# Turning x on TensorE instead of the DMA, half of r too, and another order and layout for the experts' loads

## The chip, the cores and the metric

The kernel runs on one core of one Trainium2 chip. The metric is device microseconds (us) of one execution. TensorE multiplies, VectorE (DVE in the profile), ScalarE (ACT) and GpSimd (POOL) do elementwise work, SyncE (SP) only issues transfers. All transfers run on the core's 16 DMA engines. A transpose of 128x128 blocks can be done in two ways here: by TensorE, which multiplies with the identity and leaves the result in PSUM, from where another engine copies it; or by a DMA transpose, which goes from SBUF to SBUF and takes 2-byte numbers only.

## The reference, cut to what matters

```python
# attention: 4 batches, 8 heads, 576 tokens, head_dim 64; only scores within tau of a row's maximum stay
scores = 1/8 * q @ k.T
attn   = softmax(where(scores >= scores.max(-1) - tau, scores, -1e9))
x      = (attn @ v)                      # put together as 2304 x 512
# a dense layer
h = x @ w_in                             # 512 -> 2048
x = maximum(0.01 * h, h) @ w_out         # 2048 -> 512
# soft mixture of 8 experts, 4 slots each
logits     = x @ phi                                     # 2304 x 32
slot_input = softmax(logits, axis=0).T @ x               # 32 x 512
slot_out[e] = maximum(slot_input[e] @ w1[e], 0) @ w2[e]  # w1: 8x512x1024, w2: 8x1024x512
out        = softmax(logits, axis=1) @ slot_out          # 2304 x 512
```

All inputs are float32 (w_in and w_out reach the chip as float64 bits and are converted there).

## The kernel before, in words

The 2304 tokens are 18 tiles of 128 rows. The program is one function, `emit`, which does not issue instructions in the order in which it names them: each step is put into a plan with a priority, one or more engines that may do it with an estimated duration, the buffers that it reads and writes, and a planner (`Plan.schedule`) lists them against modelled engines, a modelled DMA and the numbered buffers of each tag. The result is one fixed order for every engine, and every engine, SP's queue too, takes its list strictly in that order: an instruction that waits holds up all behind it.

Per tile, `attention(t)` loads q, computes the scores of eight heads on TensorE (L1089), takes the row maximum on DVE (L1102), the exponential on ACT (L1123), the threshold on DVE (L1130), and splits the result into a high and a low float16 half (ACT L1156, POOL L1166). Eight DMA transposes per tile (L1188, 9 blocks of 128 columns each) turn this into `aT`, and TensorE multiplies it with v (L1198) into the PSUM tile `X`.

Then comes the part that is changed. DVE divides X into `x32` (L1220, float32). ACT makes its float16 half (L1228), DVE or POOL the rest (L1231), and one DMA transpose of 8 blocks (L1238) makes `xT`. `feed(t)` multiplies xT with w_in in four chunks j of 512 columns (L1266, 12 matmuls each, into the PSUM tag `h`, which has two buffers). ACT applies the leaky ReLU (L1279) and makes the float16 half of `r[j]` (L1285), POOL or DVE the rest (L1288), and a DMA transpose of 8 blocks (L1311) makes `rT[j]`. TensorE multiplies the four rT[j] with w_out times phi (L1321, L1325) into the logits. `block` takes two tiles at a time and adds their share to the softmax over the tokens (L1381 to L1505). So a tile issues 8 + 1 + 4 = 13 DMA transposes, all of them on SP's queue, 234 in the whole run. From 100 to 545 us of the span this is the work of all engines; before it weights are converted, after it come the last two tiles and the experts.

The experts are bound to loads. `load` puts a piece of 256 KB into any free buffer of a large pool (tag list `CH`, many tags that the tiles use before). For w1 (L1702) a piece is 128 rows of 512 columns, a row of 2 KB; four experts write the four quarters of the partitions of one PSUM tile `h1`, in the order expert j outside, row block k inside. For w2 (L1773) a piece is 2 x 128 rows of half of the columns, 256 floats or 1 KB in a run; here expert j is already inside. There are 64 pieces of each. The output is made in two column halves `hf`, each after its 32 pieces of w2: evict (L1783), spread (L1786, L1789, L1791), 18 matmuls (L1802), evictions (L1809 on ACT, L1812 on DVE) and nine stores (L1820), each with runs of 1 KB. Stores of the first half are kept back in the plan until the last load is issued.

Of the kernel before, what the change touches and what calls it, by code (L numbers as in the profile page):

```python
# [341 lines left out]
def emit(tc, a, out, dbg=None, opt=None):  # L342
# [2 lines left out]
    ctx = ExitStack()  # L345
    pl = Plan()
    O = dict(
        LH=2.3, LB=2.6, HG=3, NR=13, NT=6, NW=5, XH=1, XT=4, KX=10, VX=5, AE=2, AH=3, AT=3, QH=2, QL=2,
        QR=2, TQ=("qr", "raw"), KR=2, VR=4, RAW=1, G=2, PO=0.3, PI=-8.0, PV=-3.0, DA=-100, TK=("kr",
        "w2"), TV=("vr", "kr"), TX=("kx", "w2"), TH=(0, 2), VP=1, MT=0, PS=0.15, NM=6, E=1, LA=2, MG=0,  # L350
        MH=0, RES=0, MI=(2, 1, 2, 1), MO=(1, 1, 1, 1), WT=("w",), PST=0, BH=1, DP={"vr": 1.0, "xT":
        0.1, "xh": 0.25, "X": -0.25, "kx": -1.0, "x32": 0.1, "g": 0.25, "E": -0.1, "S": -1.0, "h": 1.0,
        "r": 1.0, "rT": 0.5, "qr": 1.0, "ql": 0.25, "qh": 1.0, "ah": 0.5, "vx": -0.1, "misc": -1.0,
        "dh": -0.25, "kr": -0.25, "z": -0.1, "th": 0.5, "aT": -1.0}, LO=4, LP=2, PB=1, TU=("x32", "xh",
        "xT", "rT"), TO=("raw", "rT"), TE=18, TR=18, TG=("g",), BI={"spa": 300}, LG=0, CAP=(("aT",
        1),), PL=-0.5, TL=("rT", "xT", "ae"), NA=24, QU=(), CT=0, CX=("aT",), TW=("aT", "ql", "qh",
        "qr"), WQ=(),
    )
# [10 lines left out]
    def t_act(n):  # L369
        return 94 + 0.832 * n  # L370
# [40 lines left out]
    for n, p_, k in (  # L411
        ("S", "pss", 2), ("X", "psx", 1), ("h", "psh", 2), ("misc", "psm", 1),
        ("r", "main", O["NR"]), ("rT", "main", O["NT"]), ("w", "main", O["NW"]),
        ("x32", "main", 1), ("xh", "main", O["XH"]), ("xT", "main", O["XT"]),
        ("qr", "main", O["QR"]), ("qh", "main", O["QH"]), ("ql", "main", O["QL"]), ("kr", "main", O["KR"]),
        ("kx", "main", O["KX"]), ("vr", "main", O["VR"]), ("vx", "main", O["VX"]),
        ("ae", "main", O["AE"]), ("ah", "main", O["AH"]), ("aT", "main", O["AT"]),
        ("z", "main", 2), ("z1", "main", 2), ("rz", "main", 2), ("nm", "main", O["NM"]),
        ("th", "main", O["NM"]), ("sm", "main", 12), ("lg", "main", 3), ("E", "main", O["E"]),
        ("dh", "main", 2), ("sl", "main", 1), ("wh", "main", 16), ("g", "main", O["G"]), ("ls", "main", 2), ("g", "main", O["G"]), ("tmp", "main", 16), ("raw", "main", O["RAW"]),  # L420
    ):
        pl.tag(n, p_, k)
# [7 lines left out]
    def dve_op(prio, ns, fn, r=(), w=()):  # L430
        return pl.add(prio, one("dve", ns, fn), r, w)
# [4 lines left out]
    def pool_op(prio, ns, fn, r=(), w=()):  # L436
        return pl.add(prio, one("pool", ns, fn), r, w)
# [15 lines left out]
    def dump(name, b, sel, prio=1e9):  # L453
# [5 lines left out]
    ident, e4, e96, ones = const([P, P]), const([P, NS]), const([P, 3, NS]), const([1, P])  # L459
    pool_op(P0, 600, lambda: make_identity(nc, ident.ap), w=[ident])  # L460
    pool_op(P0, 150, lambda: pool.memset(ones.ap, 1.0), w=[ones])
    dve_op(
        P0, 250,
        lambda: dve.tensor_reduce(
# [672 lines left out]
    def attention(t):  # L1137
# [5 lines left out]
        for pr in range(4):  # L1143
# [40 lines left out]
            for i in range(2):  # L1184
# [58 lines left out]
        return xT, xh  # L1243

# [7 lines left out]
    def feed(t, xT, xh):  # L1252
# [4 lines left out]
        for j in range(4):  # L1257
# [37 lines left out]
            else:  # L1295
# [13 lines left out]
            dma_t(  # L1309
                p + 0.1, 8,  # L1310
                (lambda j: lambda: sp.dma_start_transpose(  # L1311
                    out=rT[j].ap, in_=r[j].ap.rearrange("p a b -> p (a b)")))(j),
                r=[r[j], wq], w=[rT[j]],
            )
# [439 lines left out]


    HC, firsts = DM // 2, []
    outv = out.rearrange("(t i p) d -> t p i d", i=2, p=P)
    so_ps = pl.buf("X", [P, 2, HC])
    for hf in range(2):
        pt = T0 + 2 + hf  # L1760
        cols = slice(hf * HC, hf * HC + HC)
        for G in range(2):
            for c in range(0, 8, 2):
                for j in range(4):
                    q = hts[G]
# [12 lines left out]

                    tail_op("pe", p, 262, f, r=[(q, (j, c // 4)), w], w=[(so_ps, j)])
# [16 lines left out]
        for t in range(0, NTILE, 2):  # L1796
# [8 lines left out]
            for i in range(2):  # L1805
# [29 lines left out]
def host(inputs):  # L1835
# [21 lines left out]

# [16 lines left out]
```

## Time and profile before

| | |
|---|---|
| median of 3 runs | 666.04 us (664.19 to 670.23) |
| profiled execution | 668.88 us |
| its span, first to last instruction | 667.1 us |
| busy in the span | PE 527.1, DVE 442.1, ACT 425.9, POOL 345.9 us |
| DMA | 145.26 MB, 316522 packets, of which 270624 under 512 B |
| mean granted TensorE clock | 0.934 of full speed |

Read it by stages: conversion of weights to about 100 us, the tiles to 545, the drain of the last two tiles and the softmax over tokens to 589, w1 to 627, w2 to 655, the last output to the end. PE is the busiest engine on average, but an average over these stages says little: what ends the waits in each stage says more.

### The profile page before, as it was taken

What the parts mean: (1) busy time and instruction counts of PE and PEld (TensorE: products, weight loads), DVE (VectorE), ACT (ScalarE), POOL (GpSimd) and SP (SyncE); (2) the same over time, 40 slices, a digit from 0 to 9 for tenths busy, and PEclk for the clock granted to TensorE, in tenths of its full rate; (3) what the DMA queues carried; (4) which work ended last, traced back from release to release, by engine and by line L of the source; (5) the groups of instructions that cost most, each with busy time, mean ns of one, the idle gap of its engine ahead of it and who ended that gap; (6) DMA issues with size and microseconds to landing.
All of it is one profiled execution on the core that took longest, in us unless ns stands there. A gap on an engine that the chain in (4) does not pass through costs nothing. (4 is left out here: it accounts for less than half of the span.)

```text
span 667.1 us, 15257 instructions
## 1 busy us (share of the span) xinstructions
PE 527.1 (79%) x5622; PEld 322.4 (48%) x5622; DVE 442.1 (66%) x1068; ACT 425.9 (64%) x806; POOL 345.9 (52%) x364
## 2 busy tenths in 40 slices
PE   0111787989799988889799989898979696499994
PEld 0011576666466545555465556565545453132553
DVE  6999978888678767878686976577776531201033
ACT  7999778776587776889677867575765542111022
POOL 3553445575676676868657877676774600000000
PEclk9999967989899999999699999799999897789998
DMA  8954889998999999999989999999998999899995
GB/s 304 338 212 123 201 227 217 249 198 183 168 192 236 190 172 186 178 211 213 182 162 189 189 155 192 207 186 168 171 156 144 256 224 242 283 381 348 365 311 196
DMA packets 316522, 145.26 MB, mean 218 GB/s; under 512 B 270624, under 2 KB 291616, under 8 KB 316448
## 3 DMA queue, kind: packets, MB, share of 16 engines
q1 hardware_dynamic: 309248, 130.56, 90.3%
q10 hardware_dynamic: 7200, 13.73, 8.3%
q8 instruction: 44, 0.72, 0.5%
q14 instruction: 30, 0.25, 0.1%
HBM read 69.27 MB, written 8.91 MB: 117 GB/s over the span
## 5 line engine op out<-in xcount | busy, mean ns | idle before, releaser
L1166 POOL TENSOR_TENSOR ah<-ae,ah 128x512 f16<-128x512 f32 (+1 forms) x216 | 206.4, 978 | 97.4 <-ACT ah L1156 72.2
L1266 PE MATMUL h<-wh,xT 128*128 128x512 f16 x864 | 217.4, 391 | 10.0 <-DMA xT<-xh 9.8
L1102 DVE TENSOR_REDUCE nm<-S 128x1 f32<-128x576 f32 x144 | 103.0, 748 | 62.7 <-PE S L1089 62.7
L1123 ACT ACTIVATE ae<-S,nm 128x576 f32<-128x576 f32 x144 | 100.8, 738 | 40.6 <-DVE nm L1102 32.9
L1266 PEld LDWEIGHTS <-xT 128*128 128x128 f16 x864 | 77.6, 101 | 91.3 <-issue 12.7
L1130 DVE SCALAR_TENSOR_TENSOR ae<-S,th,ae 128x576 f32<-128x576 f32 x144 | 113.7, 812 | 11.1 <-ACT ae L1123 10.3
L1198 PE MATMUL X<-vx,aT 128*128 128x64 f16 (+1 forms) x2240 | 94.2, 200 | 30.0 <-DMA aT<-ah 29.9
L1198 PEld LDWEIGHTS <-aT 128*128 128x128 f16 (+1 forms) x2240 | 82.4, 105 | 62.8 <-DMA aT<-ah 41.7
L1156 ACT ACTIVATE ah<-ae 128x576 f16<-128x576 f32 x144 | 96.0, 681 | 10.5 <-DVE ae L1130 8.9
L1089 PE MATMUL S<-kx,qh 64*128 64x288 f32 (+1 forms) x600 | 82.4, 340 | 6.8 <-DVE ae L1130 6.2
L1279 ACT ACTIVATE g<-h 128x512 f32<-128x512 f32 x72 | 42.9, 596 | 49.5 <-PE h L1266 42.7
L1089 PEld LDWEIGHTS S<-kx,qh 64*128 64x128 f32 (+1 forms) x600 | 56.0, 199 | 25.9 <-issue 21.5
L1288 POOL TENSOR_TENSOR r<-g,r 128x512 f16<-128x512 f32 x42 | 48.8, 1166 | 17.1 <-ACT r L1285 17.1
L1089 PE MATMUL S<-kx,ql 64*128 64x288 f32 (+1 forms) x280 | 48.3, 316 | 11.2 <-DVE ql L975 11.2
L1285 ACT ACTIVATE r<-g 128x512 f16<-128x512 f32 x72 | 45.0, 628 | 0.4
L1288 DVE TENSOR_TENSOR r<-g,r 128x512 f16<-128x512 f32 x30 | 28.9, 965 | 20.1 <-ACT r L1285 20.1
L1089 PEld LDWEIGHTS S<-kx,ql 64*128 64x128 f32 (+1 forms) x280 | 32.3, 202 | 11.6 <-DVE ql L975 11.6
L496 PE MATMUL misc<-c,tmp 128*1 128x128 f32 x16 | 4.5, 380 | 33.4 <-DVE tmp L563 30.0
L1321 PE MATMUL misc<-c,rT 128*128 128x64 f16 x288 | 19.0, 190 | 9.5 <-DMA rT<-r 9.5
L1321 PEld LDWEIGHTS <-rT 128*128 128x128 f16 x288 | 17.5, 97 | 12.2 <-DMA rT<-r 10.0
L799 PE MATMUL misc<-c,w 128*128 128x32 f32 x128 | 19.3, 298 | 4.4 <-DVE w L791 2.6
L1231 POOL TENSOR_TENSOR xh<-x,xh 128x512 f16<-128x512 f32 x12 | 14.4, 1200 | 15.3 <-ACT xh L1228 12.6
(334 smaller groups left out, 828.8 us busy)
## 6 DMA issues: line engine op xcount, KB each, us to landing
wh<-in_w SPq DMA_DIRECT2D x29, 256.0 KB, 6.4
r<-in_w SPq DMA_DIRECT2D x24, 256.0 KB, 5.2
rT<-in_w_out SPq DMA_DIRECT2D x22, 256.0 KB, 3.5
ah<-in_w_in SPq DMA_DIRECT2D x9, 512.0 KB, 5.9
kx<-in_w SPq DMA_DIRECT2D x16, 256.0 KB, 5.9
ae<-in_w_in SPq DMA_DIRECT2D x7, 512.0 KB, 4.3
vr<-in_v SPq DMA_DIRECT2D x10, 320.0 KB, 4.1
scr<-w SPq DMA_DIRECT2D x12, 256.0 KB, 3.9
```

Of the source, the lines that this page charges most:

```text
L1089: pe.matmul(out=pss[i].ap[:rows, n, :HALF], lhsT=l.ap[64 * i : 64 * i + 64, pr, :rows], rhs=m.ap[64 * i : 64 * i + 64, n * HALF : (n + 1) ...
L1102: lambda: dve.tensor_reduce(out=nm.ap, in_=ps.ap[:, :, :HALF], axis=AX.XY, op=ALU.max, negate=True),
L1123: lambda: act.activation(out=e(), in_=ps.ap[:, :, :HALF], func=AF.Exp, bias=nm.ap[:, 0:1], scale=1.0),
L1130: lambda: dve.scalar_tensor_tensor(out=e(), in0=ps.ap[:, :, :HALF], scalar=th.ap[:, 0:1], in1=e(), op0=ALU.is_ge, op1=ALU.mult, accum_out= ...
L1156: (lambda ah, ae, i: lambda: act.activation(out=ah.ap[:, i, :S], in_=ae.ap[:, i], func=AF.Copy))(ah, ae, i),
L1166: (lambda ah, ae: lambda: pool.tensor_tensor(out=ah.ap[:, h, w0 : w0 + c1 - c0], in0=ae.ap[:, h, c0:c1], in1=ah.ap[:, h, c0:c1], op=ALU.su ...
L1198: pe.matmul(out=X.ap[r0:r1, 2 * pr + i], lhsT=aT.ap[:, c, r0:r1], rhs=vtiles[b, pr].ap[:, wv, cv], start=(pr == 0 and i == 0 and n == 0), ...
L1266: pe.matmul(out=hp.ap, lhsT=xT.ap[:, wx * 4 + k], rhs=wh[k][j].ap[:, ww], start=(n == 0), stop=(n == 11),)
L1279: (lambda g, hp: lambda: act.activation(out=g.ap, in_=hp.ap, func=AF.Prelu, alpha=0.01))(g, hp),
L1285: (lambda j, g: lambda: act.activation(out=r[j].ap[:, 0], in_=g.ap, func=AF.Copy))(j, g),
L1288: fg = lambda eng, j, g: lambda: eng.tensor_tensor(out=r[j].ap[:, 1], in0=g.ap, in1=r[j].ap[:, 0], op=ALU.subtract)
L1321: pe.matmul(out=L.ap, lhsT=rT[j].ap[:, c], rhs=wq.ap[:, 4 * j + c], start=(j == 0 and c == 0), stop=False,)
```

## The change

Four edits:

1. `x32` gets a second buffer, the float16 pair `xh` goes, and TensorE turns x32 itself, as float32, in four 128x128 transposes into a PSUM tile of tag `h`. ACT copies it to the high half of xT, DVE subtracts to get the low half; both now read PSUM and write xT directly.
2. Of the four chunks of r, chunks 1 and 3 (`RJ`) are turned by TensorE (8 float16 transposes of 128x128 into a tile of tag `h` (`XP`), then two copies of 512 columns on ACT or DVE); chunks 0 and 2 still go by DMA transpose. A tile then has 10 DMA transposes in place of 13: 18 + 36 = 54 fewer in the run.
3. For w1 the loops are swapped: k outside, expert j inside, for the loads and for the matmuls.
4. The host lays w2 out so that a piece has 128 rows of 2 KB, and the output so that a store has 128 rows of 2 KB; the host turns the output back.

```diff
-        xh, xT = pl.buf("xh", [P, 2, DM], F16), pl.buf("xT", [P, 8, P], F16)
-        act_op(
-            p, t_act(512), lambda: act.activation(out=xh.ap[:, 0], in_=x32.ap, func=AF.Copy),
-            r=[x32], w=[(xh, 0)],
-        )
...
-        add_alt(p, [("dve", P2(t_dve(512)), fx(dve)), ("pool", t_pool(512), fx(pool))], r=[x32, (xh, 0)], w=[(xh, 1)])
-        att_last.append(
-            dma_t(
-                p, 8,
-                lambda: sp.dma_start_transpose(out=xT.ap, in_=xh.ap.rearrange("p a b -> p (a b)")),
-                r=[xh], w=[xT],
-            )
...
+        xp, xT = pl.buf(O["XP"], [P, 4, P], F32, "xp"), pl.buf("xT", [P, 8, P], F16)
+
+        def f():
+            for k in range(4):
+                pe.transpose(xp.ap[:, k], x32.ap[:, k * P : (k + 1) * P], ident.ap)
+
+        pe_op(p, 440, f, r=[x32, ident], w=[xp])
         act_op(
+            p, 490, lambda: act.activation(out=xT.ap[:, 0:4], in_=xp.ap, func=AF.Copy), r=[xp],
+            w=[(xT, 0)],
+        )
+        dve_op(
+            p, 602,
+            lambda: dve.tensor_tensor(
+                out=xT.ap[:, 4:8], in0=xp.ap, in1=xT.ap[:, 0:4], op=ALU.subtract
+            ),
+            r=[xp, (xT, 0)], w=[(xT, 1)],
         )
...
+            if j in O["RJ"]:
+
+                rp = pl.buf(O["XP"], [P, 8, P], F16, "rp")
...
+                        pe.transpose(rp.ap[:, c], r[j].ap[:, c // 4, c % 4 * P : c % 4 * P + P], ident16.ap)
+
+                pe_op(p + 0.1, 8 * 56, f, r=[r[j], ident16, wq], w=[rp])
+                for i in range(2):
+                    add_alt(
...
+                            ("act", 490, (lambda j, i, rp: lambda: act.activation(
+                                out=rT[j].ap[:, 4 * i : 4 * i + 4], in_=rp.ap[:, 4 * i : 4 * i + 4],
+                                func=AF.Copy))(j, i, rp)),
+                            ("dve", 602, (lambda j, i, rp: lambda: dve.tensor_copy(
...
+                        r=[rp], w=[(rT[j], i)],
+                    )
+            else:
+                dma_t(
+                    p + 0.1, 8,
...
-            for j in range(4):
-                e = 4 * G + j
-                for k in range(4):
+            for k in range(4):
+                for j in range(4):
+                    e = 4 * G + j
...
-                        a["w2"][4 * G + j, c * P : (c + 2) * P, cols].rearrange("(k p) d -> p k d", p=P),
-                        T0 - 7, [P, 2, HC],
+                        a["w2"][hf, 4 * G + j, c // 2].rearrange("p (k d) -> p k d", k=2), T0 - 7, [P, 2, HC]
...
-                    out=outv[t // 2, :, :, cols], in_=ot.ap))(t, ot, cols),
+                    out=out[hf, t // 2], in_=ot.ap.rearrange("p i d -> p (i d)")))(t, ot, hf),
```

## Rows read from the trace of the kernel before

**Rows 1.** Busy us (and instructions) per stretch: PE, weight loads, DVE, ACT, POOL; clock, DMA, GB/s.

```profile
400.00:500.00 100.00, 88.37 (x1142) 55.87 (x1138) 70.55 (x165) 67.65 (x124) 72.00 (x77) 0.97 1.06 180
545.00:589.00 44.00, 28.92 (x196) 12.87 (x195) 8.25 (x23) 10.99 (x23) 0.35 (x1) 0.80 1.02 275
589.00:627.00 38.00, 38.00 (x150) 11.37 (x149) 3.15 (x5) 4.82 (x9) 0.00 (x0) 0.96 1.08 362
627.00:655.00 28.00, 26.92 (x292) 17.19 (x291) 7.43 (x29) 4.12 (x10) 0.00 (x0) 1.00 0.91 307
```

**Rows 2.** Waits of PE from 100 to 545: total us, times, longest.

```profile
PE X L1198 <- DMA aT<-ah: 29.9, 30, 2.5
PE h L1266 <- DMA xT<-xh: 9.8, 6, 3.3
```

**Rows 3.** Chain of waits from 470 to 545: shares by line; one piece (start, us).

```profile
by line: PE h L1266 26.4%; DMA aT<-ah 20.2%; issue 9.9%; POOL ah L1166 9.6%; PE X L1198 9.0%; DMA xT<-xh 7.0%; POOL r L1288 4.6%; PE S L1089 3.6%; PE misc L1494 1.9%; PE misc L1321 1.6%; POOL xh L1231 1.5%; SPq L1188 1.5%; ACT ah L1156 0.9%
...
493.42 5.27 DMA xT<-xh
```

**Rows 4.** SP's queue: issue ns min/median/max; and its longest wait, 100 to 545.

```profile
L1238 SPq DMA_TRANSPOSE xT<-xh x18: 1231/1252/3459, 112.9 to 541.1; - x18
...
L1311 SPq DMA_TRANSPOSE rT<-r x72: 1231/1342/4691, 175.8 to 568.2; - x72
...
SPq L1188 <- POOL ah L1166: 72.0, 47, 3.6
```

**Rows 5.** Groups by line and shape: copies of 128x512 out of PSUM.

```profile
L789 ACT ACTIVATE w<-h 128x512 f32<-128x512 f32 x9 | 5.4, 598 | 5.6 <-PE h L783 5.6
...
L791 DVE COPY w<-h 128x512 f32<-128x512 f32 x7 | 4.8, 688 | 3.3 <-PE h L783 3.2
```

**Rows 6.** Instructions in order of time on PE (start, us): prices of matmuls in a row.

```profile
487.51 0.58 PE L1198 MATMUL X<-vx,aT 128*128 128x64 f16 x14 [1.15 <-DMA aT<-ah]
...
543.23 10.53 PE L1266 MATMUL h<-wh,xT 128*128 128x512 f16 x48
...
627.11 0.60 PE L1715 MATMUL h<-c,ql 128*128 128x128 f32 x4
```

**Rows 7.** The drain: two pieces of the chain, and r's last low half.

```profile
551.38 7.62 DMA rT<-r
...
564.19 6.75 DMA rT<-r x2
...
567.47 0.69 DVE L1288 TENSOR_TENSOR r<-g,r 128x512 f16<-128x512 f32 x1 [3.34 <-ACT r L1285]
```

**Rows 8.** Instructions in order of time on PE, at w1 and at w2.

```profile
612.12 0.59 PE L1702 MATMUL S<-r,aT 128*32 128x512 f32 x1
612.15 0.59 PE L1702 MATMUL S<-wh,aT 128*32 128x512 f32 x1
612.58 0.59 PE L1702 MATMUL S<-rT,aT 128*32 128x512 f32 x1
...
628.09 0.38 PE L1773 MATMUL X<-kr,ae 128*32 128x256 f32 x1
628.11 0.38 PE L1773 MATMUL X<-vr,ae 128*32 128x256 f32 x2
628.20 0.38 PE L1773 MATMUL X<-w,ae 128*32 128x256 f32 x1
```

**Rows 9.** SP's issues of the experts' loads, 41st, 65th and last of 128; issue to landing.

```profile
577.90 1.04 SPq L1690 DMA_DIRECT2D wh<-in_w  x2
...
593.59 0.38 SPq L1690 DMA_DIRECT2D kr<-in_w  x1
...
640.49 0.37 SPq L1690 DMA_DIRECT2D kr<-in_w  x1
...
DMA to landing us min/median/max: 2.8/5.6/7.2
```

**Rows 10.** After the last matmul of w2: its eviction, the start of the output.

```profile
654.43 0.38 ACT L1783 ACTIVATE aT<-X 128x256 f32<-128x256 f32 x1 [4.43 <-PE X L1773]
```

More of the change, by code (lines that the diff above doesn't have):

```diff
@@ L353, in emit @@
         "r": 1.0, "rT": 0.5, "qr": 1.0, "ql": 0.25, "qh": 1.0, "ah": 0.5, "vx": -0.1, "misc": -1.0,
-        "dh": -0.25, "kr": -0.25, "z": -0.1, "th": 0.5, "aT": -1.0}, LO=4, LP=2, PB=1, TU=("x32", "xh",
-        "xT", "rT"), TO=("raw", "rT"), TE=18, TR=18, TG=("g",), BI={"spa": 300}, LG=0, CAP=(("aT",
+        "dh": -0.25, "kr": -0.25, "z": -0.1, "th": 0.5, "aT": -1.0}, LO=4, LP=2, PB=1, TU=("x32", "xT",
+        "rT"), TO=("raw", "rT"), TE=18, TR=18, TG=("g",), BI={"spa": 300}, LG=0, CAP=(("aT",
         1),), PL=-0.5, TL=("rT", "xT", "ae"), NA=24, QU=(), CT=0, CX=("aT",), TW=("aT", "ql", "qh",
@@ L413, in emit @@
         ("r", "main", O["NR"]), ("rT", "main", O["NT"]), ("w", "main", O["NW"]),
-        ("x32", "main", 1), ("xh", "main", O["XH"]), ("xT", "main", O["XT"]),
+        ("x32", "main", O["NX"]), ("xT", "main", O["XT"]),
         ("qr", "main", O["QR"]), ("qh", "main", O["QH"]), ("ql", "main", O["QL"]), ("kr", "main", O["KR"]),
@@ L461, in emit @@
     pool_op(P0, 150, lambda: pool.memset(ones.ap, 1.0), w=[ones])
+    ident16 = const([P, P], F16)
+    dve_op(P0, 150, lambda: dve.tensor_copy(out=ident16.ap, in_=ident.ap), r=[ident], w=[ident16])
     dve_op(
@@ L568, in floats_of @@
         return ws, pow2_of(prio, hw)
-    pl.early.update(("raw_in", "raw_out"))
+    pl.early.update(("raw_in", "raw_out", "xp", "rp"))
     if O["WT"] != ("w",):
@@ L725, in emit @@
     for k in range(4):
-        w32, pk = floats_of(PW, a["w_in"], k, (S23, ("x32", "rT", "xh", "xT"), "raw_in"))
+        w32, pk = floats_of(PW, a["w_in"], k, (S23, ("x32", "rT", "xT"), "raw_in"))
         sk = scale_from(PW + 0.16, pk, 4.0)
@@ L1225, in attention @@
         )
-        xh, xT = pl.buf("xh", [P, 2, DM], F16), pl.buf("xT", [P, 8, P], F16)
+        xp, xT = pl.buf(O["XP"], [P, 4, P], F32, "xp"), pl.buf("xT", [P, 8, P], F16)
[3 more added lines that the diff above has]
+        pe_op(p, 440, f, r=[x32, ident], w=[xp])
         act_op(
-            p, t_act(512), lambda: act.activation(out=xh.ap[:, 0], in_=x32.ap, func=AF.Copy),
-            r=[x32], w=[(xh, 0)],
-        )
-        fx = lambda eng: lambda: eng.tensor_tensor(
-            out=xh.ap[:, 1], in0=x32.ap, in1=xh.ap[:, 0], op=ALU.subtract
-        )
-        add_alt(p, [("dve", P2(t_dve(512)), fx(dve)), ("pool", t_pool(512), fx(pool))], r=[x32, (xh, 0)], w=[(xh, 1)])
-        att_last.append(
-            dma_t(
-                p, 8,
-                lambda: sp.dma_start_transpose(out=xT.ap, in_=xh.ap.rearrange("p a b -> p (a b)")),
-                r=[xh], w=[xT],
-            )
+            p, 490, lambda: act.activation(out=xT.ap[:, 0:4], in_=xp.ap, func=AF.Copy), r=[xp],
+            w=[(xT, 0)],
+        )
+        dve_op(
[4 more added lines that the diff above has]
+            r=[xp, (xT, 0)], w=[(xT, 1)],
         )
         dump(f"x{t}", x32, lambda q: q)
-        return xT, xh
+        return xT, None
     acc, accx = const([P, 512]), const([P, P]) if wlq else None
@@ L1308, in feed, with f @@
                 )
[L1309 to L1314, printed above, removed]
+            if j in O["RJ"]:
+                rp = pl.buf(O["XP"], [P, 8, P], F16, "rp")
+                def f(j=j, rp=rp):
+                    for c in range(8):
+                        pe.transpose(rp.ap[:, c], r[j].ap[:, c // 4, c % 4 * P : c % 4 * P + P], ident16.ap)
+                pe_op(p + 0.1, 8 * 56, f, r=[r[j], ident16, wq], w=[rp])
+                for i in range(2):
+                    add_alt(
+                        p + 0.1,
+                        [
+                            ("act", 490, (lambda j, i, rp: lambda: act.activation(
+                                out=rT[j].ap[:, 4 * i : 4 * i + 4], in_=rp.ap[:, 4 * i : 4 * i + 4],
+                                func=AF.Copy))(j, i, rp)),
+                            ("dve", 602, (lambda j, i, rp: lambda: dve.tensor_copy(
+                                out=rT[j].ap[:, 4 * i : 4 * i + 4], in_=rp.ap[:, 4 * i : 4 * i + 4]
+                            ))(j, i, rp)),
+                        ],
+                        r=[rp], w=[(rT[j], i)],
[3 more added lines that the diff above has]
+                    p + 0.1, 8,
+                    (lambda j: lambda: sp.dma_start_transpose(
+                        out=rT[j].ap, in_=r[j].ap.rearrange("p a b -> p (a b)")))(j),
+                    r=[r[j], wq], w=[rT[j]],
+                )
         p = base + O["LB"] - O["LH"]
@@ L1599, in emit @@
     T0 = NTILE + 10.0
-    CH = ("wh", "kx", "kr", "vr", "vx", "qr", "r", "rT", "w", "w2", "raw", "xh", "xT", "x32") + O["CX"]
+    CH = ("wh", "kx", "kr", "vr", "vx", "qr", "r", "rT", "w", "w2", "raw", "xT", "x32") + O["CX"]
     TW = O["TW"]
@@ L1846, in host @@
     va = np.concatenate([vf, np.concatenate([vl, vl], axis=2)], axis=3)
+    w2 = np.asarray(inputs["moe2_w2"]).reshape(8, 4, 2, P, 2, DM // 2)
+    w2a = w2.transpose(4, 0, 1, 3, 2, 5).reshape(2, 8, 4, P, DM)
     def bits(w):
@@ L1853, in host @@
         "w_out": bits(inputs["moe_w_out"]), "phi": np.asarray(inputs["moe2_phi"]),
-        "w1": np.asarray(inputs["moe2_w1"]), "w2": np.asarray(inputs["moe2_w2"]),
+        "w1": np.asarray(inputs["moe2_w1"]), "w2": w2a,
     }
@@ L1868 @@
     }
-    out = nc.dram_tensor("out", (NT, DM), F32, kind="ExternalOutput").ap()
+    out = nc.dram_tensor("out", (2, NTILE // 2, P, DM), F32, kind="ExternalOutput").ap()
     with tile.TileContext(nc) as tc:
@@ L1872 @@
     r = run_bass_kernel_spmd(nc, [{"in_" + n: x for n, x in arr.items()}], core_ids=[0])
-    return r.results[0]["out"]
+    y = r.results[0]["out"].reshape(2, NTILE // 2, P, 2, DM // 2)
+    return np.ascontiguousarray(y.transpose(1, 3, 2, 0, 4)).reshape(NT, DM)
```

9 lines of the change are left out of this document (3 added, 6 removed).

## The prediction, made before the changed kernel was run

> **What bounds it now.** I read the busy times by stretch first, then who waits for whom, then the chain of waits backward, then single instructions where a price is needed. Three stretches matter. While the tiles run (100 to 545) no engine is full: PE 88%, DVE 71, ACT 68, POOL 72 [rows 1]. PE's idle time there has almost one cause: 39.7 us end with the landing of a DMA transpose, aT for 29.9 and xT for 9.8 [rows 2]. SP's queue, on the other hand, waits for POOL's low halves [rows 4]. So the tiles go round in a loop: matmul, evict, split, transpose on the one in-order DMA queue, matmul again. The chain shows the shares of that loop from 470 to 545: PE's lines 42.5% (26.4 + 9.0 + 3.6 + 1.9 + 1.6), aT's landing 20.2, xT's 7.0, POOL 15.7, and ACT and DVE under 1 [rows 3]. In the drain (545 to 589) PE is busy 28.9 of 44 us, and the two longest pieces of the chain are landings of rT [rows 1, 7]. From 589 to 654 PE never rests (38.0 of 38, then 26.9 of 28) while the DMA moves 362 and 307 GB/s [rows 1]. The last load is issued at 640.49 and takes about 5.6 to land, 646.1 [rows 9], yet w2's last matmul ends at 654.4 [rows 10]: in the experts PE is behind the loads.
>
> **The change, step by step.** *New work on PE.* 18 x 4 float32 transposes: four of that shape take 0.60 [rows 6], so 72 x 0.15 = 10.8 us. 36 x 8 float16 transposes of 128 columns have no row. With 64 columns one costs 0.041 (0.58/14), with 512 columns 0.219 (10.53/48) [rows 6]; a quarter of the latter is 0.055, and I take 0.06, so 17.3 us. The ends are 0.041 (11.8) and the float32 price 0.15 (43). Together 28 us (23 to 54), and as PE holds 42.5% of the loop, +12 of it on the path.
>
> *x without the DMA.* In the chain one pass through x costs 6.4 us, 8.5% of 75 (DMA 5.27 and POOL's xh 1.5%) [rows 3]. In its place come 0.60 on PE, a copy of 0.60 on ACT and a subtraction of about 0.69 on DVE [rows 5, 6], 1.9 in all. That is 4.5 a pass, and with six such stretches in 445 us up to -26. The loop has other sides that are nearly as long (POOL's ah and r, and the issue gaps, are 24% of it), so I take half, -13. What is late next is x32 itself, then POOL's ah.
>
> *SP's queue.* 18 x 1.25 + 36 x 1.34 = 71 us of issuing go from it [rows 4], and with them 54 of 234 transposes, 23%. If aT's landings shrank in proportion, 0.202 x 445 x 0.23 = -21; if POOL's halves set them [rows 4], nothing. I take half, -10.
>
> *ACT, DVE, POOL.* 72 copies of 512 columns from PSUM, 0.60 on ACT or 0.69 on DVE [rows 5]: shared evenly 21.5 and 24.8 us. The subtraction for x goes to DVE alone, 18 x 0.69 = 12 more there at most, and POOL loses it. DVE rises by 37 us in 445, from 71 to about 79% of the stretch. On the chain both are under 1% [rows 3]; of the 37 I take under a tenth, +3 (0 to +37). The PSUM tag h with its two buffers gets 54 more users; I count nothing for it, the cover being PE's 88%.
>
> Tiles: 12 - 13 - 10 + 3 = **-8**, bounds -25 and +20.
>
> *Drain.* r's last low half is done at 568.16, and the last landing that L waits for comes at 570.94 [rows 7]. With chunk 3 on PE: 8 x 0.06 + 0.60 and two handovers, 569.5, so -1.5. The long landing before it (7.62) is chunk 2's, which stays with the DMA; fewer transposes around it, -1. **-2.5** (0 to -7).
>
> *w1.* Each piece is two PE instructions. Now two run side by side: starts at 612.12 and 612.15, the next at 612.58, thus 0.43 for two [rows 8], and 128 of them 27.5 us. At w2, where j is already inside, four streams start within 0.11 (two in the row with x2) [rows 8]. With four quarters at work w1 takes 13.8. PE then catches up with the loads, and the DMA sets the end: 646.1 + 0.9 for the last piece = 647.0 in place of 654.4, -7.4.
>
> *w2 in rows of 2 KB.* The 24 w1 issues from 577.90 to 593.59 are 0.654 apart, the 63 of w2 from there on 0.744 [rows 9]. If the run length is the reason, the last load lands 63 x 0.09 = 5.7 earlier, if not, 0; I take -4, as both paces hold while the DMA is full [rows 1].
>
> The Trainium skill has a rule against this term: DMA: Bandwidth & Descriptors, Specifications, gives 512 B as the smallest transfer at line rate, so that runs of 1 KB should already have it and the term would be 0; no run here yet shows which.
>
> *Clock and output.* Where PE has waits (545 to 589) its granted clock is 0.80 of full, where it has none 1.00 [rows 1]. Waiting for loads it may drop to the lower level in the last matmuls: +1 (0 to +2). The rest after w2, 654.4 to 667.1, is eviction and stores at ACT's and DVE's pace; stores in rows of 2 KB change nothing there. The first half's stores then run beside that chain; nine at the loads' pace take 6 us, and the first store of the second half comes 3 to 4 after w2's end, so they are nearly through: 0. Experts: -7.4 - 4 + 1 = **-10.5** (-5 to -13).
>
> **Sum.** -8 - 2.5 - 10.5 = -21. The profiled execution took 668.9 (span 667.1 and 1.8 around it), 2.8 above the median of the runs. 668.9 - 21 = 647.9, so 645 beside the median of 666.0.
>
> **Rivals.** *PE becomes the bound (slower).* PE's list is in strict order. So far SP's queue waited for r's and x's halves; now PE does, with the scores and matmuls of the next tiles behind it, whose ends DVE's maximum and ACT's g wait for. Price: all 28 us of work on the path and 54 waits of 0.3, 16 more, against -13 and -10: tiles +21, so 674. It decides from +20 in the tiles. For it: PE's 88%. Against it: PE's idle time ends with DMA landings, and at 0.041 for a short matmul much of the 88% is the tail of single instructions. 0.11. Half of it (tiles +6 to +20) ends within 1%: 0.08.
>
> *The tiles stay as they are.* New work and saved landings cancel; drain and experts alone give 653. For it: aT's landings, three times xT's share, remain. 0.15.
>
> *The experts hang on loads as slow as now.* Runs of 1 KB are not the reason for 0.744, and the clock falls: experts -5.5, so 650. 0.10.
>
> *The swap does nothing.* If PE keeps two streams at a time, the tail gains 0: 655. Against it: w2's rows. 0.04.
>
> *Transposes do not overlap.* Float16 ones then cost 0.15 like the float32 ones, 26 more, 11 on the path: 656. Against it: four in 0.60, with 64 columns 0.041. 0.04, half of it within 1%.
>
> The Trainium skill goes further, in TensorE: Matmul & The Clock Gate, Part 4: about 275 ns for a 128x128 transpose inside a kernel; 360 of them would be 99 us, where 0.15 each for the float32 ones in a row speaks against adding up such durations.
>
> **Chances and range.** The forecast has 0.48, with a range of its own from 631 to 657. Under 1% can't be told from no change here, so faster means below 659.4: 0.48 + 0.15 + 0.10 + 0.04 + 0.02 = 0.79. Within 1%: 0.08 + 0.02 = 0.10. Slower: 0.11. The range from 628 to 662 takes in a tile stretch of -25 and all cases but the slower one, part of those within 1%, and some 0.05 below.
>
> **What will show it.** Waits of L1266 for a DMA must be gone, and waits of PE for aT shorter than 29.9; if they are gone while PE waits for DVE's x32 or r's low halves, the first rival is right. DVE near 79% of the tile stretch. At w1 four PE starts per 0.43 and PE idle between pieces of w2; the last load's landing then lies within 2 us of w2's last matmul. Issues of w2's loads 0.65 to 0.68 apart say that the run length counted, 0.74 that it did not. I am wrong if the tiles' end does not come earlier, or if the experts' gain is not at least 5 us.

## The result and the profile after

The changed kernel takes 631.7 us (median of 4 runs, 628.47 to 633.91) where the kernel before takes 668.13 on the same chip (median of 4, 664.19 to 670.52): ratio 0.9456, interval 0.9388 to 0.9525. The forecast of 645 had the sign and most of the mechanisms, and 631.7 lies inside its range; the time fell 13 us further. The profiled execution of after took 628.47 with a span of 626.7, so it is the fastest of its four: of the 40.4 us between the two spans, about 4 are scatter between executions. The points below are read from the two traces and cut the whole span into stretches.

| us of the span | before | after | stretch before | stretch after | moved | forecast |
|---|---|---|---|---|---|---|
| last division into x32 starts | 537.7 | 522.2 | 537.7 | 522.2 | -15.5 | -8 (tiles) |
| last matmul with w_in ends | 566.1 | 541.7 | 28.4 | 19.5 | -8.9 | -2.5 (drain) |
| w1's first matmul | 589.8 | 564.3 | 23.7 | 22.6 | -1.1 | 0 |
| w2's last matmul ends | 654.3 | 613.9 | 64.5 | 49.6 | -14.9 | -10.5 (experts) |
| end of the span | 667.1 | 626.7 | 12.8 | 12.8 | 0 | 0 |

Two rows of this table hang on the single execution behind each trace. e_xr, f_w2old and f_noorder (below) differ from the changed kernel only behind the tiles and give every engine the same instructions in the same order up to w1; their last x32 starts at 528.6, 522.8 and 531.6, where the changed kernel has 522.2. What spreads these four over 9.4 us is not known, so the tiles' -15.5 may be anything from -6 to -15.5. And e_tail, which has the order of the kernel before through tiles and drain, needs 22.6 us for the second row where the kernel before has 28.4.

First the busy times by stretch of the kernel after; columns as in [rows 1].

```profile
400.00:500.00 100.00, 94.94 (x1256) 61.73 (x1253) 74.55 (x179) 74.87 (x136) 71.27 (x83) 1.00 0.88 157
...
564.00:582.00 18.00, 18.00 (x150) 5.68 (x148) 3.15 (x5) 4.67 (x9) 0.00 (x0) 1.00 1.05 389
582.00:614.00 32.00, 31.36 (x291) 18.74 (x289) 7.36 (x29) 3.88 (x9) 0.00 (x0) 1.00 1.04 390
```

PE went from 88 to 95 of 100 us in the tiles, with the granted clock at 1.00 in place of 0.97. w1 has shrunk from 37 us to 18 with the same 128 expert matmuls, and in w2 the DMA moves 390 GB/s in place of 307: PE no longer lags behind the loads there.

Waits of PE, then of SP's queue, 100 to 545, after (total us, times, longest):

```profile
PE X L1198 <- DMA aT<-ah: 17.1, 19, 2.4
```
```profile
SPq L1188 <- POOL ah L1166: 115.0, 49, 6.9
```

The wait for aT fell from 29.9 to 17.1 and that for xT's landing (9.8) is gone [rows 2]. SP's queue now waits more for POOL's halves, 115.0 in place of 72.0 [rows 4]: it is empty more often. How little room that gives is shown by the experiments.

What the new operations cost, after, by line and shape (busy us, mean ns of one | idle before):

```profile
L1231 PE MATMUL h<-c,x 128*128 128x128 f32 x72 | 12.2, 296 | 0.2 <-ACT rT L1325 0.2
L1318 PE MATMUL h<-c,r 128*128 128x128 f16 x288 | 22.1, 219 | 3.0 <-DVE rT L1328 1.4 <-ACT r L1288 1.4 <-DVE r L1291 0.3
L1325 ACT ACTIVATE rT<-h 128x512 f16<-128x512 f16 x36 | 21.0, 593 | 11.9 <-PE h L1318 9.3 <-DVE rT L1328 2.6
L1328 DVE COPY rT<-h 128x512 f16<-128x512 f16 x36 | 14.7, 419 | 8.7 <-PE h L1318 4.8 <-ACT rT L1325 3.8
```

Busy time of PE holds the tail of single instructions; the marginal price comes from an experiment below. The drain, PE in order of time, after (start, us):

```profile
526.07 5.34 PE L1269 MATMUL h<-wh,xT 128*128 128x512 f16 x24
...
533.61 4.69 PE L1269 MATMUL h<-wh,xT 128*128 128x512 f16 x21
538.14 0.61 PE L1318 MATMUL h<-c,r 128*128 128x128 f16 x8
538.99 2.75 PE L1269 MATMUL h<-wh,xT 128*128 128x512 f16 x12 [0.24 <-ACT g L1282]
```

The last tile's matmuls with w_in run through, with 0.24 us of waiting. Before, the same list stopped inside the last tile, because the logits of the tile before (L1321) stood ahead in PE's order and waited for the landing of 7.62 [rows 7]; three such waits made 8.7 us between 545 and 590. After, one is left:

```profile
PE misc L1347 <- DMA rT<-r: 2.5, 1, 2.5
```

Only the first of the three waits lies ahead of the last matmul with w_in. It and the matmuls behind it, in the kernel before and then in e_tail, which has the same order here:

```profile
559.04 0.23 PE L1321 MATMUL misc<-c,rT 128*128 128x64 f16 x1 [4.64 <-DMA rT<-r]
...
559.38 6.75 PE L1266 MATMUL h<-wh,xT 128*128 128x512 f16 x18
```
```profile
555.88 0.20 PE L1321 MATMUL misc<-c,rT 128*128 128x64 f16 x1 [1.60 <-DMA rT<-r]
...
556.11 4.04 PE L1266 MATMUL h<-wh,xT 128*128 128x512 f16 x18
```

Before, the wait is 3.0 longer and the 18 matmuls behind it take 2.7 longer; after the 4.64 us without work the granted clock is 0.58 of full from 559.38 to 566, mostly its lower level (1.2 GHz), where e_tail has 1.00 (2.4 GHz) in its 4.04 us.

w1 on PE after, which answers to [rows 8]:

```profile
580.62 0.59 PE L1728 MATMUL S<-kr,aT 128*32 128x512 f32 x1
580.63 0.59 PE L1728 MATMUL S<-vr,aT 128*32 128x512 f32 x1
580.63 0.59 PE L1728 MATMUL S<-w,aT 128*32 128x512 f32 x1
580.64 0.59 PE L1728 MATMUL S<-kx,aT 128*32 128x512 f32 x1
581.05 0.59 PE L1728 MATMUL S<-kr,aT 128*32 128x512 f32 x1
```

Four starts within 0.02 us and the next ones 0.43 later, where it was two per 0.43. Last, SP's 65th and last issue of the experts' loads, and the eviction after w2's last matmul, after:

```profile
564.14 0.33 SPq L1716 DMA_DIRECT2D kx<-in_w  x1
...
607.58 0.33 SPq L1716 DMA_DIRECT2D aT<-in_w  x1
```
```profile
614.00 0.38 ACT L1806 ACTIVATE ql<-X 128x256 f32<-128x256 f32 x1 [5.03 <-PE X L1796]
```

Issues of w2's loads are 43.44 / 63 = 0.690 us apart (0.744 before [rows 9]). The last one lands at 612.8 and w2 ends 1.1 later; before, it ended 8.1 after the last landing.

### The profile page after: what moved, and what is told of

Its sections match the earlier page's. It is cut to its first block, busy times and chain, and to the rows that moved or that the text cites. A ratio compares the mean times of both kernels' runs of the same rounds, so it can differ in the third digit from the quotient of the medians.

```text
span 626.7 us, 15895 instructions
## 1 busy us (share of the span) xinstructions
PE 518.7 (83%) x5982; PEld 336.3 (54%) x5982; DVE 450.5 (72%) x1085; ACT 443.4 (71%) x841; POOL 344.0 (55%) x385
## 4 chain that ended last, share of the span: by engine, by line
PE 42%; DMA 24%; DVE 12%; POOL 9%; ACT 8%; issue 4%; SPq 1%; ACTq 0%; POOLq 0%; DVEq 0%
PE h L1269 15%; DMA aT<-ah 14%; PE S L1089 7%; PE X L1198 7%; POOL ah L1166 6%; PE X L1796 3%; PE S L1728 2%; DVE ae L1130 2%; DMA ae<-in_w_in 2%; DVE w L642 2%; DVE nm L1102 2%; PE misc L801 2%; PE h L1318 1%; ACT ah L1156 1%; POOL r L1291 1%
## 5 line engine op out<-in xcount | busy, mean ns | idle before, releaser
L1166 POOL TENSOR_TENSOR ah<-ae,ah 128x512 f16<-128x512 f32 (+1 forms) x216 | 201.3, 956 | 100.2 <-ACT ah L1156 76.8
L1269 PE MATMUL h<-wh,xT 128*128 128x512 f16 x864 | 210.7, 380 | 2.8 <-ACT rT L1325 1.2
L1123 ACT ACTIVATE ae<-S,nm 128x576 f32<-128x576 f32 x144 | 101.6, 736 | 29.8 <-DVE nm L1102 25.3
L1198 PE MATMUL X<-vx,aT 128*128 128x64 f16 (+1 forms) x2240 | 92.0, 198 | 18.4 <-DMA aT<-ah 17.1
L1089 PE MATMUL S<-kx,qh 64*128 64x288 f32 (+1 forms) x620 | 80.3, 333 | 2.5 <-DVE ae L1130 2.4
L1291 POOL TENSOR_TENSOR r<-g,r 128x512 f16<-128x512 f32 x49 | 57.4, 1171 | 17.0 <-ACT r L1288 15.9
L1325 ACT ACTIVATE rT<-h 128x512 f16<-128x512 f16 x36 | 21.0, 593 | 11.9 <-PE h L1318 9.3
L1291 DVE TENSOR_TENSOR r<-g,r 128x512 f16<-128x512 f32 x23 | 19.0, 828 | 14.2 <-ACT r L1288 14.2
L1318 PE MATMUL h<-c,r 128*128 128x128 f16 x288 | 22.1, 219 | 3.0 <-DVE rT L1328 1.4
L801 PEld LDWEIGHTS misc<-c,w 128*128 128x128 f32 x128 | 19.7, 228 | 4.9 <-DVE w L793 2.0
L1115 POOL TENSOR_SCALAR th<-nm,c 128x1 f32<-128x1 f32 x49 | 13.6, 281 | 15.1 <-DVE nm L1102 11.0
```

The costliest lines, as they stand in the source:

```text
L801: pe.matmul(out=wpp.ap, lhsT=wt.ap[:, k], rhs=phi.ap[:, k], start=(k == 0), stop=(k == 3))
L1089: pe.matmul(out=pss[i].ap[:rows, n, :HALF], lhsT=l.ap[64 * i : 64 * i + 64, pr, :rows], rhs=m.ap[64 * i : 64 * i + 64, n * HALF : (n + 1) ...
L1123: lambda: act.activation(out=e(), in_=ps.ap[:, :, :HALF], func=AF.Exp, bias=nm.ap[:, 0:1], scale=1.0),
L1166: (lambda ah, ae: lambda: pool.tensor_tensor(out=ah.ap[:, h, w0 : w0 + c1 - c0], in0=ae.ap[:, h, c0:c1], in1=ah.ap[:, h, c0:c1], op=ALU.su ...
L1198: pe.matmul(out=X.ap[r0:r1, 2 * pr + i], lhsT=aT.ap[:, c, r0:r1], rhs=vtiles[b, pr].ap[:, wv, cv], start=(pr == 0 and i == 0 and n == 0), ...
L1269: pe.matmul(out=hp.ap, lhsT=xT.ap[:, wx * 4 + k], rhs=wh[k][j].ap[:, ww], start=(n == 0), stop=(n == 11),)
```

## Experiments

Changes between kernels of different groups are taken from the medians; by the ratios to the kernel before, which each group has its own runs of, they come out between 1 us smaller and 4 us larger, and both are given where it matters. A difference between two kernels of this section is uncertain by some 6 us even so: f_noorder has e_xr's instructions in e_xr's order and the better layout of w2 and the output, and yet took 652.6 where e_xr took 649.11.

### The parts alone

Edits 3 and 4 alone (e_tail), edit 1 alone (e_x), edit 2 alone (e_r), edits 1 and 2 (e_xr), each put into the kernel before.

```text
e_tail:  w1's loops swapped, w2 and output in rows of 2 KB
e_x:     x32 turned by TensorE, xh gone
e_r:     RJ=(1, 3)
e_xr:    e_x and e_r
```

> The kernel before with edits 3 and 4 alone (w1 with the expert inside, w2 and output in rows of 2 KB). My theory, that the parts add up: tiles and drain stay (last x32 at 538, w1 begins at 590), w1 takes 17 us in place of 37, w2 ends 1 us after its last load lands, in all -11 to -15 us, ratio 0.978 to 0.984. Rival, that the end hangs on when the loads could begin, which edits 1 and 2 moved: the loads still end at 642 to 646, so -7 at most, ratio 0.99.

> The kernel before with edit 1 alone (x32 turned by TensorE, 18 DMA transposes fewer). Theory A, the loop through x is what the tiles wait for: the last x32 comes 10 to 15 us earlier, ratio 0.978 to 0.985, drain unchanged. Theory B, the gain goes by the number of transposes taken from SP's queue (18 of 54): a third of the 25 us that tiles and drain gained together, -8, ratio 0.988. Theory C, that it needs both edits because one alone only moves the wait: 0 to -4.

> The kernel before with edit 2 alone (chunks 1 and 3 of r turned by TensorE, 36 DMA transposes fewer). Theory A: r is not on the loop of the tiles, so the last x32 comes at the same time within 4 us, and only the drain gets shorter, by 5 to 10 us, ratio 0.985 to 0.993. Theory B: two thirds of the 25 us, -17, ratio 0.975, with the last x32 10 us earlier. Theory C: 0 to -4.

> The kernel before with edits 1 and 2, the experts as before. If the parts add up: last x32 at 522, w1 begins at 548, then the old 77 us, in all -25 us, ratio 0.963. If the loads' start is what edits 1 and 2 give and the old w1 order hides it: w1 and w2 remain 64 us long behind an earlier start, the same -25; if instead PE in w1 had caught up only through the new order, more than 64 us between the start of w1 and the end of w2, ratio 0.975 or more.

| | us | ratio, interval | last x32 | to last w_in matmul | to w1 |
|---|---|---|---|---|---|
| e_tail | 654.69 | 0.981, 0.9762 to 0.9858 | 537.6 | 22.6 | 25.1 |
| e_x | 641.74 | 0.9628, 0.9579 to 0.9677 | 524.6 | 14.9 | 25.0 |
| e_r | 658.41 | 0.9868, 0.9823 to 0.9912 | 535.3 | 19.1 | 25.5 |
| e_xr | 649.11 | 0.9728, 0.9686 to 0.9771 | 528.6 | 19.6 | 25.7 |

The before of these runs had 666.64 (median of 7). Edit 1 is worth 25 us, more than any theory expected, and edit 2 alone is worth 8. Together they give 17.5, less than edit 1 alone. A gain in proportion to the transposes taken from SP's queue is refuted by this: 18 fewer give 25, 36 fewer 8, 54 fewer 17.5.

Where the gains lie is less plain than the table looks. The column from the last x32 to the last w_in matmul measures above all how much work the planner's order leaves there: 83 matmuls with w_in start behind the last x32 in the kernel before and in e_tail, 72 in e_r, 65 in e_xr and the changed kernel, 49 in e_x, at 0.22 us each [rows 6]. From e_tail to e_x that is 34 x 0.22 = 7.5 of the 7.7 us: work that the order puts ahead of x32, not a wait that is gone. Tiles and drain are best taken together. The last w_in matmul ends at 566.1 before and at 560.2 in e_tail, at 539.5 in e_x, 554.4 in e_r and 548.2 in e_xr. Of the drain in e_x, PE's waits for rT from 524 to 564, and its matmuls with w_in:

```profile
PE misc L1324 <- DMA rT<-r: 5.7, 3, 3.2
```
```profile
527.71 3.63 PE L1269 MATMUL h<-wh,xT 128*128 128x512 f16 x16 [0.24 <-DVE xT L1240]
532.83 6.64 PE L1269 MATMUL h<-wh,xT 128*128 128x512 f16 x30
```

xT is there about 3 us after x32 started (524.6 to 527.7); before, it landed 9 us after (537.7 to 546.65). PE did not stand for that last landing: it had 48 matmuls with w_in in a row from 543.23 on [rows 6].

### Without r's edit, and in another order

f_xtail is the changed kernel with all of r by DMA transpose; f_plan has all four edits, but other assumed durations in the planner, which thereby lists the work in another order and gives some of it to another engine: DVE makes 32 of r's 72 low halves in place of 23, POOL 40 in place of 49.

```diff
 f_xtail: edits 1, 3 and 4, not 2
 f_plan:
-            p, 490, lambda: act.activation(out=xT.ap[:, 0:4], ...
+            p, 560, lambda: act.activation(out=xT.ap[:, 0:4], ...
-            p, 602,
+            p, 690,
```

> x on TensorE, w1's loops swapped and w2 and the output in rows of 2 KB, but all four chunks of r by DMA transpose. Alone, x gave 25 us and the experts' two edits 12. Theory A (the parts add, r's edit gives nothing more): 627 to 631, no slower than all four edits together (631.7), last x32 at about 525 of the span. Theory P (the gain of the tiles comes from transposes taken out of SP's queue, so r's 36 are missed): 640 or more, last x32 at 530 or later.

> All four edits, the work is the same; only the planner's assumed durations of xT's copy and subtraction are raised (490 to 560, 602 to 690), so that it lists the instructions in another order. Theory 'the order is worth several us': the time moves by 4 to 10 us either way from 631.7, with last x32 moved by as much from 522. Theory 'the order is worth nothing, edits 1 and 2 alone differ from all four in their tiles for another reason': within 2 us, last x32 at 522 plus or minus 1.5.

f_xtail took 630.76 (ratio 0.9435, 0.9383 to 0.9486; 6 runs), not to be told from the changed kernel (0.9456): it beats the kernel before by as much, with one edit less. The parts multiply: 0.9628 x 0.981 = 0.9445. f_plan took 637.63 (0.9548, 0.9483 to 0.9614), 6 us above the changed kernel (0.9388 to 0.9525). That is no proof that the changed kernel's order is a good draw: the intervals overlap, f_plan's last x32 (529.6) lies within the 522.2 to 531.6 that one and the same order took in four kernels, and e_xr, which has that order, multiplies with e_tail to 0.9543, the same 6 us above. r's edit on top of x's is worth between nothing (f_xtail) and a loss of 7 (e_x to e_xr), which is hardly more than that scatter. PE's waits of f_xtail, 100 to 545:

```profile
PE X L1198 <- DMA aT<-ah: 19.4, 21, 3.1
```

With 36 more transposes in the queue PE waits 19.4 for aT, only 2.3 more than after.

### The price of TensorE's work

Same order, each TensorE transpose issued twice.

```diff
-            for k in range(4):
+            for k in 2 * list(range(4)):
...
-                    for c in range(8):
+                    for c in 2 * list(range(8)):
```

> All four edits in the same order of instructions, but each transpose by TensorE (x's and r's) is issued twice: the same result written again. That is the work on TensorE of the transposes a second time, an estimate of 28 us of it. Theory L (TensorE's new work lies mostly beside waits, 42% of it on the path as in the prediction): 12 us slower, 640 to 648. Theory 'TensorE has room': at most 4 us slower. Theory 'TensorE is the bound by now': 20 us slower or more, 652.

645.65 (0.9649, 0.9587 to 0.9712), 14 us more (13 by the ratios). By line and shape:

```profile
L1318 PE MATMUL h<-c,r 128*128 128x128 f16 x576 | 38.1, 219 | 2.1 <-ACT r L1288 1.4 <-DVE rT L1328 0.4 <-DVE r L1291 0.3
...
L1231 PE MATMUL h<-c,x 128*128 128x128 f32 x144 | 20.4, 288 | 0.2 <-ACT rT L1325 0.2
```

The second time costs PE 38.1 - 22.1 = 16.0 us for r (0.056 each) and 20.4 - 12.2 = 8.2 for x (0.114 each), 24.2 together; 14 / 24.2 = 0.58 of it is on the path, in these single kernels. The prediction had 28 us and 0.425, so 12: the run agrees within its uncertainty.

### The price of a place in SP's queue

f_dma54 is the changed kernel, g_dma18 is f_xtail; both keep the order and get more DMA transposes of 3 blocks into a spare tile.

```diff
 f_dma54 and g_dma18, for one aT of each tile:
-  sp.dma_start_transpose(out=aT.ap, in_=ah.ap[:, i])
+  [sp.dma_start_transpose(out=aT.ap, in_=ah.ap[:, i]), again(ah.ap[:, i, : 3 * P]) if pr + i == 0 else None]
 f_dma54 only, for each rT:
-  out=rT[j].ap, in_=r[j].ap.rearrange("p a b -> p (a b)"))
+  out=rT[j].ap, in_=r[j].ap.rearrange("p a b -> p (a b)")) and again(r[j].ap[:, 0, : 3 * P])
```

> All four edits in the same order, with 54 more DMA transposes of 3 blocks of 128x128 on SP's queue, right behind the 36 of r and behind one of aT's per tile, into a spare tile that nothing reads: as many transposes as before, 234, each added one with 3/8 of the blocks. Theory P (the queue's issue time and the transposes' share of the DMA were the price): 54 x 1.2 us of issuing come back, and at least 10 us of it on the path: 641 or more, waits of PE for aT back from 17 towards 30 us. Theory L (the gain came from the shorter way of x and not from the queue): at most 5 us slower, 632 to 637.

> x on TensorE and the experts' edits, r all by DMA transpose (630.8), in the same order, with 18 more DMA transposes of 3 blocks, one per tile behind the first of aT, into a spare tile that nothing reads: SP's queue has as many transposes as before x was taken from it. Theory Q (each transpose more in SP's queue costs 0.7 us of time, as the 54 did: 39 us / 54): 13 us slower, 642 to 646, so that half of x's 25 us is the queue. Theory X (x's gain is its shorter way; the 54 cost so much because 36 of them stood behind r's, in front of aT's): at most 4 us slower, 631 to 635.

f_dma54 took 670.61 (1.0039, 0.9992 to 1.0085): 39 us more, the whole gain. g_dma18 took 653.37 (0.9831, 0.9756 to 0.9905): 22.6 us over f_xtail, 26 by the ratios. g_dma18 lies beyond what either theory expected; f_dma54 fits "at least 10 us", with longer waits for aT than the 30 us named there. PE's wait for aT in f_dma54, 100 to 545:

```profile
PE X L1198 <- DMA aT<-ah: 41.2, 37, 5.1
```

The same view of g_dma18, and its added instructions (ns min/median/max):

```profile
PE X L1198 <- DMA aT<-ah: 29.7, 29, 2.5
```
```profile
L895 SPq DMA_TRANSPOSE spare<-ah x18: 1247/1282/2765, 72.8 to 517.9; - x18
```

The 18 behind aT cost 22.6 / 18 = 1.26 us each, about all of their 1.28 us of issuing, although SP's queue waits 80 us for POOL's halves in f_xtail. The 36 behind rT are left with 39 - 22.6 = 16, 0.45 each, if the two kernels' prices add; up to 4.6 us of that are waits of the added transposes for each other's landing. The rival, that the added bytes slow the DMA down, can be looked up in the time from aT's issue to its landing, 100 to 545 (us); first the changed kernel and f_dma54, then f_xtail and g_dma18:

```profile
DMA to landing us min/median/max: 3.2/3.7/7.4
DMA to landing us min/median/max: 3.2/3.7/7.4
```
```profile
DMA to landing us min/median/max: 3.2/3.9/7.7
DMA to landing us min/median/max: 3.2/3.9/7.1
```

Once issued, aT lands as fast as without them. So it is the queue's order: aT's transposes stand behind, and are issued 1.28 later each. PE's waits for aT are not the whole of it. From 100 us to the last x32, f_xtail and then g_dma18:

```profile
100.00:522.00 422.00, 390.92 (x4801) 251.60 (x4798) 329.74 (x780) 319.69 (x594) 299.94 (x336) 0.98 1.02 190
100.00:541.00 441.00, 399.24 (x4818) 255.66 (x4818) 333.45 (x783) 322.72 (x600) 300.15 (x336) 0.96 1.02 187
```

Of these 19 us more, 10.3 are waits for aT (29.7 in place of 19.4), and 8.3 are PE busy longer with the same work, at a granted clock of 0.96 in place of 0.98.

So the 18 that edit 1 takes away are worth up to 23 of its 25 us. How much of this belongs to their old place (behind xh, not behind aT) stays open.

### The price of r's copies

The changed kernel in the same order, each copy of r's turned half issued twice.

```diff
-  lambda: act.activation(out=rT[j].ap[:, 4 * i : 4 * i + 4], ...)
+  lambda: [act.activation(out=rT[j].ap[:, 4 * i : 4 * i + 4], ...) for _ in range(2)][1]
 (and so for dve.tensor_copy)
```

> All four edits in the same order, but each copy of r's turned half out of PSUM (36 on ACT, 36 on DVE) is issued twice: 36 x 0.59 + 36 x 0.42 = 36 us more work on the two engines. Theory 'beside': the copies lie beside TensorE's work as the prediction had it (under a tenth), at most 4 us slower. Theory 'on the path': the matmul that reads rT and PSUM's h buffers wait for them, 10 us slower or more, which with the 14 us that the doubled TensorE work cost would be what eats the queue's gain from r.

653.52 (0.9823, 0.9729 to 0.9917), 22 us more (24 by the ratios). By line and shape, and PE's waits from 100 to 545:

```profile
L1325 ACT ACTIVATE rT<-h 128x512 f16<-128x512 f16 x72 | 42.6, 596 | 17.4 <-PE h L1318 8.3 <-DVE rT L1328 5.8 <-PE S L1089 1.3
L1328 DVE COPY rT<-h 128x512 f16<-128x512 f16 x72 | 30.0, 423 | 15.2 <-ACT rT L1325 7.9 <-PE h L1318 5.5
```
```profile
PE h L1269 <- ACT rT L1325: 3.6, 2, 1.8
PE h L1231 <- ACT rT L1325: 3.4, 2, 2.0
PE h L1269 <- DVE rT L1328: 3.3, 2, 2.1
```

36.9 us of work (42.6 - 21.0 and 30.0 - 14.7), 0.6 of it on the path. Part of it is the PSUM tag h: PE's next matmuls and transposes wait for its two buffers until the copies are done, 10.3 us in these rows. What the rest consists of is not shown.

### The experts' edits, taken back one at a time

```diff
 f_noorder:
-            for k in range(4):
-                for j in range(4):
-                    e = 4 * G + j
+            for j in range(4):
+                e = 4 * G + j
+                for k in range(4):
 f_w2old:
-  a["w2"][hf, 4 * G + j, c // 2].rearrange("p (k d) -> p k d", k=2), T0 - 7, [P, 2, HC]
+  a["w2"][4 * G + j, c * P : (c + 2) * P, cols].rearrange("(k p) d -> p k d", p=P), T0 - 7, [P, 2, HC]
```

> All four edits, but w1's loops as before (expert outside, row block inside), the rest of the order unchanged. Theory B (TensorE runs two streams in place of four, w1 takes 37 us and not 17.4, and w2 behind it takes its own 27): w2's end at 564 + 37 + 1 + 27 = 629 of the span in place of 614, so 15 us slower, 646 to 648. Theory D (the loads set the experts' end in either order): at most 3 us slower, w2 ends within 2 us of the last landing.

> All four edits, but w2 in its old layout, pieces with runs of 1 KB; the output keeps its rows of 2 KB. Theory R (the run length sets the pace of w2's loads): landings 0.745 to 0.75 apart in place of 0.688, the last 63 x 0.06 = 4 us later, 3.5 to 5 us slower, 635 to 637. Theory 'something else sped the loads': landings 0.69 apart, within 1.5 us of 631.7.

f_noorder took 652.6 (0.9821, 0.9726 to 0.9916): 21 us more, beyond the 646 to 648 that were expected. Its profiled execution is the longest of its four, and reaches w1 13 us later than the changed kernel with the same order of instructions, so only its own stretches are read. w1 and w2:

```profile
578.00:615.00 37.00, 37.00 (x143) 10.57 (x142) 3.15 (x5) 4.35 (x8) 0.00 (x0) 0.96 1.05 391
615.00:643.00 28.00, 27.13 (x292) 17.32 (x291) 7.34 (x29) 4.25 (x10) 0.00 (x0) 1.00 0.48 178
```

and PE at w1:

```profile
599.95 0.59 PE L1728 MATMUL S<-r,aT 128*32 128x512 f32 x1
600.35 0.59 PE L1728 MATMUL S<-wh,aT 128*32 128x512 f32 x1
600.38 1.05 PE L1728 MATMUL S<-r,aT 128*32 128x512 f32 x3
```

w1 takes 37.2 us again, one or two streams at a time, and the DMA runs dry in w2 (178 GB/s): the last load lands at 623.1 and w2 ends 19.6 later. w1 start to w2 end is 65.0 in place of 49.6, which gives the swap 15 us in the kernel after, twice the forecast's 7.4.

f_w2old took 636.07 (0.9576, 0.9498 to 0.9654), 4.4 us more (8 by the ratios). SP's 65th and last issue:

```profile
566.26 0.38 SPq L1716 DMA_DIRECT2D kx<-in_w  x1
...
612.62 0.37 SPq L1716 DMA_DIRECT2D aT<-in_w  x1
```

46.36 / 63 = 0.736 us apart. All kernels here with runs of 1 KB have 0.73 to 0.75 between landings of w2's loads (f_w2old, e_x, e_r, e_xr and before), all with 2 KB 0.67 to 0.70: the run length is the reason. By its pace it is worth 63 x 0.046 = 3 us; the rest of the 4.4 is within the scatter.

## Why the prediction came out as it did

**Tiles, -8 against -15.5.** TensorE's work was sized right: 24.2 us, 14 on the path (forecast 28 and 12). Two terms were wrong in opposite directions, so that the sum came as near as it did is in part luck. The step "if POOL's halves set them, nothing. I take half, -10" failed: the queue's waits for POOL were read as slack. They are not: the 54 cost 39 us when added in f_dma54, because aT's transposes are issued later by each one ahead of them. The step "of the 37 I take under a tenth, +3" failed too: r's copies alone cost 22 a second time. The chain's share of ACT and DVE (under 1% [rows 3]) told who ended last there, not what happens when PSUM's buffers are held longer. A copy of float16 takes DVE only 0.42 us where 0.69 was taken from float32 [rows 5]; the stretch's DVE share is 77% (344 of 445), forecast 79, but the forecast added its 37 us to the 71% of 400 to 500: over the whole stretch DVE was at 74% before (331 of 445) and rose by 13 us. What x's shorter way (-13) gives beside its place in the queue is not separated. The 15.5 are of single executions: the same order of instructions ends the tiles 6 to 15.5 us earlier, with -8 inside.

**r's edit.** The same prices have the sign of what it gives beside x's: the queue's 16, against 9 (16.0 x 0.58) on TensorE and 22 for the copies, so a loss of 15 where 0 to 7 was measured. An addition that the planner does not know falls in a place that it did not choose, so each of these is rather an upper bound; the sign agrees with e_xr.

**Drain, -2.5 against -10.** Of the 28.4 us in the trace before, 5.8 are one longer landing and the lower clock behind it, which e_tail with the same order does not have. Against e_tail's 22.6 the changed kernel's 19.5 is -3, about as forecast, and the step to w1 (22.6, where e_xr and f_w2old have 25.7 and 25.3) moved by no more than these kernels differ among themselves. The forecast gave x nothing here. In e_x the stretch is 7.7 shorter than in e_tail, but by the 34 matmuls that its order no longer leaves there; that is the tiles' end, seen at another instruction. So most of the -10 is not a term that the prediction missed, and its own reason (chunk 3 of r, -1.5, and fewer transposes around the long landing, -1) is not tested part by part.

**Experts, -10.5 against -14.9.** By parts: PE's lag behind the last landing went from 8.1 to 1.1, so -7.0 (forecast -7.4); 63 issues closer by 0.054, -3.4 (forecast -4); the 65th load is issued 0.1 us ahead of w1's start where it was 3.8 behind, -3.9 (not in the forecast); landing 0.5 sooner. w1 itself took 17.4 us where the working had 13.8: its price of two streams per 0.43 gives 27.5 for the old order, which took 36.9, because in part of the time only one ran (starts at 606.93, 607.36, 607.79 and 608.22 one by one; [rows 8] show a piece with two). It did not matter, since the loads set the end. The clock did not drop (1.00 from 564 to 614; forecast +1; the forecast's 1.00 where PE does not wait passes over the 0.96 of 589 to 627 [rows 1]). The end is set by the loads, within 2 us as said. The output took 12.8 both times, as forecast.

The Trainium skill's rule that runs from 512 B on have line rate (DMA: Bandwidth & Descriptors, Specifications) does not hold for this term: 0.736 us from one piece of 256 KB to the next with 1 KB, 0.690 with 2 KB. Nor do the 275 ns that the Trainium skill gives for a transposition (TensorE: Matmul & The Clock Gate, Part 4) add up here: the marginal 24.2 us over 360 are 67 ns each.

**Rivals.** PE as the bound: no, though it is near (95%), and in f_pe2 further work costs about half of itself. Tiles unchanged: no. Loads as slow as now: only with 1 KB runs (f_w2old). The swap does nothing: no (f_noorder). Transposes that do not overlap: 0.056 each, no.

## What to carry to other kernels

In an in-order queue, count an instruction that stands ahead of what the path needs at up to its full issue time, even where the queue shows long waits: waits at its head are no slack for what stands behind. Before calling a stage shorter, look at how much work the order leaves in it, and at a second kernel with the same order there: here that took 5.8 us of the drain and up to 9 of the tiles out of what could be read as an effect. Where two resources run close (PE and the loads in the experts), an edit is worth what it gives until the other binds: the swap was worth 15 us once the loads came earlier.

## What the runs showed of the hardware

Matmuls that fill different 32-column quarters run side by side as far as their order lets them: with eight instructions in a row to one quarter (four row blocks of two) one or two ran at a time, and 128 took 37.2 us; with two in a row, and the quarters in turn, mostly three or four ran, and 128 took 17.4, evictions included. The Trainium skill (TensorEngine Tiling (Array Packing), Key Properties) says that such tiles work independently; the trace agrees for instructions that stand near each other in the order. And loads of 256 KB in 256 runs of 1 KB are not as fast as in 128 runs of 2 KB: 0.736 and 0.690 us from one issue to the next, 6%.
